# Bounds of the attention scores: one head per partition by way of DRAM instead of matmuls, a shift for each head, and a planner's allowance of 1.88

## The chip, the cores and the metric

The kernel runs on one NeuronCore of one Trainium2 chip. The metric is the device time of one execution in microseconds (us). Before the change three runs gave 1153.82, 1157.62 and 1160.69 us; the median is 1157.62 us. The core has five engines with a queue each: TensorE (PE in the profile, with its weight loads shown apart as PEld), VectorE (DVE), ScalarE (ACT), GpSimd (POOL) and SyncE (SP). An engine works through its own queue strictly in order. DMA transfers are issued from SP, POOL and ACT.

## The reference

Two independent layers are computed and their outputs are put side by side. A is a long convolution (an S4 layer); B is attention with 32 query heads that share one key and one value head.

```python
# A: u is 2048 x 576, 128 states per channel
K = einsum("dn,dnl,dn->dl", C, exp(dt * A * l), dt * B).real
ya = irfft(rfft(u, 4096) * rfft(K, 4096))[:2048] + u * Dskip
# B: x is 2048 x 576, H = 32 heads of 18
q = (x @ wq).reshape(2048, 32, 18)
k, v = x @ wk, x @ wv                 # 2048 x 18 each, shared by all heads
p = softmax(einsum("qhd,kd->hqk", q, k) * 18 ** -0.5)
yb = einsum("hqk,kd->qhd", p, v).reshape(2048, 576) @ wo
out = concatenate([ya, yb], axis=-1)
```

## The kernel before

**Attention** sets the frame. The 2048 queries are cut into 4 chunks c of 512; in a chunk come 8 groups g of 4 heads, in a group 16 blocks kb of 128 keys, and in a block two head pairs. That makes 1024 tiles of scores; two tiles (one key block of four heads) are called a step, so there are 512 steps, and a round of the main loop (`main`) takes three tiles. For each tile PE makes the scores `s` (L516) from a stacked fp16 query tile `aug` and the keys `kaug`, ACT turns them into `P = exp(s)` (L527, and L525 in the first group), and PE adds `P` times the values to `ops` (L823). At the end of a group DVE copies `ops` to `o`, which goes to DRAM as `od`; later it is divided by its sums and multiplied with `wo` (`op`, `outproj`, and at the very end `fin` in `finish`). A fin product that has not been started when the last scores are done is computed in `finish`, after the loop.

**Queries.** For each chunk five units m of up to 128 columns of `wq` (7, 7, 7, 7 and 4 heads) are projected on PE (`q`, L408). DVE splits the result into two fp16 halves `qh` and `ql` and takes the largest magnitude per column over the 512 queries, `ab` (L135). POOL stores the halves to the DRAM tensor `qd` (L458), from which SP fetches head pairs into the five `aug` buffers (L505).

**Bounds.** Softmax needs a shift that keeps exp in range. For a head, the sum over its 18 dimensions of max|q| times max|k| bounds every score. Before the change these sums run over partitions, since `ab` has a column of q per partition, and are done on PE: DVE builds a 128 x 128 tile `aw` out of `ab` and the key maxima `kmax` (L127), PE multiplies it with a 0/1 table `sel` into the PSUM tile `up` (L193; 8, 16 or 24 matmul records a unit), DVE reduces it to `un` (L135), takes the running maximum `u` over all units so far (L119), and spreads it into `sh`, which POOL stores as row 54 of `qd` (L496). All heads of a unit thus get one shift: the largest bound of any head so far. `kmax` itself comes from six instructions of PE and two of DVE in `bounds` (L374 to L387), called after round 2 of the main loop. The largest bound of all decides at the end, through `flag`, whether a slower general branch has to run.

**Convolution.** Its 576 channels are worked off in 12 pieces: DVE makes tables (`fr`, `tab`, L119 and L123), PE contracts them (`kg`, L1259) and transforms u and the kernel (`hu`, `lu`, `hk`, `lk`, `iy`, all L193), DVE multiplies (`us`, `ks`, `acc`, `pt`) and writes the result. Three times ACT computes a batch of sines and exponentials (`stage`).

**What sets the order.** PE, ACT and DVE run in the order in which the program was written, and a planner writes it: a `Clock` with estimated costs keeps one time for each of the three engines, and generators for the queries and bounds (`side`), the normalisation (`prepare`) and the convolution (`Conv`) yield what they want next: "v" for DVE work, "p" for PE work, in either case with the time from which it may go, and "w" to wait. `fill` puts pieces of such work between the attention's matmuls while a credit lasts. All PE pieces of this kind write to one single PSUM bank (`ps_f`, given out by `bank`), which the next piece can take only when DVE has read the last. `RATE` (1.84) is how many microseconds of the convolution's DVE work are allowed per step, `PACE` (1.79) the pace below which the convolution goes ahead of the queries. SP's and POOL's orders are made by a scheduler afterwards.

Two details matter for what follows. The first unit of chunk 0 is projected in `setup`, and its bounds wait until `bounds` has been called. The second one is projected in the main loop, after the bounds of the first.

## Time and profile before

| | |
|---|---|
| runs shown | 1153.82, 1157.62, 1160.69 us (median 1157.62) |
| profiled execution | 1154.84 us, of which the span from the first to the last instruction is 1153.0 us |
| granted TensorE clock, mean | 0.994 |
| busy in the span | PE 1080.8 us, ACT 998.7 us, DVE 995.5 us, POOL 141.4 us |
| DMA | 83.37 MB, mean 72 GB/s |

The page gives for each engine its busy time and share of the span. PE's busy time has modelled ends, so it is not work at PE's peak. A group line reads: line, engine, operation, output<-inputs, sizes, count | busy us in total, mean ns of one | idle time of the engine just before them, and what ended it. In the waits a row reads: who waited <- for whom: us in total, times, longest. A row of the timeline reads: start, duration, engine, line, operation, tiles, count, and in brackets the idle time before it with its cause; SPq is SP's queue issuing DMAs. All times are us from the start of the span.

### The profile page before, as it was taken

Reading aid. Unit: us, or ns where it says so; the run is one execution under the profiler, and the core shown is the slowest. Engines: PE = TensorE matmul, PEld = TensorE weight load, DVE = VectorE, ACT = ScalarE, POOL = GpSimd, SP = SyncE. Lnnn points to the kernel's source line nnn. Section 1 sums busy time; section 2 is a strip of 40 time slices with the busy share of each in tenths; the row PEclk is TensorE's granted clock in tenths of the full one; section 3 lists DMA queues with packets and bytes.
Section 4 is the critical chain, followed back from the end, with each engine's and each line's share of the span. In section 5 each row is a group of like instructions: output and inputs, shape, how many; then the busy total and the mean of one; then the engine's idle time right before and its main releaser. Section 6 shows DMA issues by size and latency. Waiting matters only on the chain.

```text
span 1153.0 us, 33069 instructions
## 1 busy us (share of the span) xinstructions
PE 1080.8 (94%) x13886; PEld 392.3 (34%) x13886; DVE 995.5 (86%) x1739; ACT 998.7 (87%) x1052; POOL 141.4 (12%) x257
## 2 busy tenths in 40 slices
PE   6999899999999999899999999999999999999998
PEld 2333323333334333324333333334323333323323
DVE  3788996998998998898899897987899899799693
ACT  3889988888888998998898999878999989899992
POOL 5320322012022000002032000001050000000000
PEclk9999999999999999999999999989999999999999
DMA  7412331114123102203122202102122200311201
GB/s 227 141 47 72 125 119 56 46 42 144 41 70 102 40 28 93 76 30 100 61 95 79 95 20 78 45 29 91 47 84 77 88 30 29 106 48 37 69 29 58
DMA packets 58895, 83.37 MB, mean 72 GB/s; under 512 B 14483, under 2 KB 34951, under 8 KB 58229
## 3 DMA queue, kind: packets, MB, share of 16 engines
q1 hardware_dynamic: 47173, 73.24, 19.4%
q0 software_dynamic: 10848, 7.37, 2.6%
q8 instruction: 111, 1.82, 0.6%
q10 hardware_dynamic: 720, 0.58, 0.2%
q14 instruction: 43, 0.35, 0.1%
HBM read 46.59 MB, written 33.85 MB: 70 GB/s over the span
## 4 chain that ended last, share of the span: by engine, by line
PE 59%; DVE 22%; ACT 11%; issue 6%; DMA 1%; SPq 0%; DVEq 0%; ACTq 0%
PE ops L823 24%; PE s L516 15%; ACT P L527 10%; PE op L193 5%; DVE tab L119 4%; PE q L408 4%; DVE ks L119 3%; PE iy L193 3%; PE kg L1259 3%; DVE acc L119 2%; DVE t L119 2%; PE hu L193 1%; DVE tt L119 1%; PE hk L193 1%; DVE fr L119 1%
## 5 line engine op out<-in xcount | busy, mean ns | idle before, releaser
L527 ACT ACTIVATE P<-s 128x1024 f32<-128x1024 f32 x992 | 934.5, 1033 | 111.9 <-PE s L516 109.7
L823 PE MATMUL ops<-P,v_sb 128*32 128x512 f32 x4096 | 508.7, 597 | 8.2 <-DVE o L123 7.8
L516 PE MATMUL s<-aug,kaug 55*128 55x512 f16 x2048 | 308.6, 382 | 37.2 <-ACT P L527 33.1
L516 PEld LDWEIGHTS <-kaug 55*128 55x128 f16 x2048 | 91.0, 94 | 371.3 <-issue 324.8
L823 PEld LDWEIGHTS ops<-P,v_sb 128*32 128x32 f32 x4096 | 116.6, 110 | 165.4 <-issue 128.4
L458 POOL DMA_DIRECT2D qd<-qh x116 | 65.6, 573 | 310.9 <-DVE qh L127 308.3
L408 PE MATMUL q<-x,wq_sb 128*32 128x256 f32 x1360 | 83.7, 382 | 0.1
L193 PE MATMUL op<-wo_sb,oT 126*32 126x288 f32 (+1 forms) x1080 | 78.5, 416 | 2.6 <-DVE ob L123 1.4
L119 DVE TENSOR_TENSOR tab<-tab,tt 128x576 f32<-128x576 f32 (+1 forms) x72 | 59.1, 821 | 1.4
L123 DVE COPY ksb<-kg 128x192 f32<-128x192 f32 x48 | 17.5, 364 | 48.2 <-PE kg L1259 48.0
L119 DVE TENSOR_TENSOR tab<-tab 128x576 f32<-128x576 f32 (+1 forms) x72 | 58.8, 817 | 0.0
L119 DVE TENSOR_TENSOR tt<-fr,sum 128x576 f32<-128x576 f32 (+1 forms) x72 | 58.8, 817 | 0.0
L119 DVE TENSOR_TENSOR tab<-fr,dif 128x576 f32<-128x576 f32 (+1 forms) x72 | 58.8, 817 | 0.0
L119 DVE TENSOR_TENSOR tab<-sum,fr 128x576 f32<-128x576 f32 (+1 forms) x72 | 58.8, 816 | 0.0
L408 PEld LDWEIGHTS q<-x,wq_sb 128*32 128x32 f32 x1360 | 39.4, 109 | 38.5 <-issue 13.7
L119 DVE TENSOR_TENSOR acc<-acc,pt 128x1728 f32<-128x1728 f32 (+2 forms) x36 | 48.6, 1351 | 0.1
L119 DVE TENSOR_TENSOR pt<-us,ks 128x1728 f32<-128x1728 f32 (+2 forms) x36 | 48.4, 1350 | 0.1
L1168 POOL MEMSET fr<- 128x192 f32 x24 | 12.0, 585 | 291.5 <-DVE tt L119 191.1
L193 PEld LDWEIGHTS op<-wo_sb,oT 126*32 126x32 f32 (+1 forms) x1080 | 30.6, 110 | 44.8 <-issue 19.1
L1259 PEld LDWEIGHTS kg<-tab 128*32 128x32 f32 x2304 | 35.8, 110 | 22.6 <-DVE ksb L123 7.6
L525 ACT ACTIVATE P<-s,bias 128x1024 f32<-128x1024 f32 x32 | 32.9, 1120 | 12.1 <-PE s L516 12.0
L1259 PE MATMUL kg<-tab 128*32 128x64 f32 x2304 | 41.7, 220 | 1.3 <-DVE tab L119 0.8
(160 smaller groups left out, 1021.0 us busy)
## 6 DMA issues: line engine op xcount, KB each, us to landing
od<-o SPq DMA_DIRECT2D x31, 256.0 KB
aug<-qd SPq DMA_DIRECT2D x124, 55.0 KB
u<-u SPq DMA_DIRECT2D x12, 384.0 KB
kd<-ksb SPq DMA_DIRECT2D x12, 384.0 KB
kt<-kd SPq DMA_DIRECT2D x48, 96.0 KB
outa<-u SPq DMA_DIRECT2D x12, 384.0 KB
pw<-pw SPq DMA_DIRECT2D x8, 528.0 KB
oT<-od SPq DMA_DIRECT2D x16, 252.0 KB
```

Of the source, the lines that this page charges most:

```text
L119: return self.v.tensor_tensor(out, *a, **k)
L123: return self.v.tensor_copy(out, *a, **k)
L193: nc.tensor.matmul(ps[j:e], w[:, j:e], x, start=start, stop=stop, tile_position=(0, j))
L408: nc.tensor.matmul(ps[o, 256 * f:256 * f + 256], w[:, k, i], xt[:, k, x], start=(k == 0), stop=(k == 4), tile_position=(0, 32 * j))
L458: q.dma_start(qd[h:h + n, row + d:row + d + nd, cs], src[i1:i1 + n * nd, :cs.stop - cs.start])
L516: nc.tensor.matmul(ps[:, j, :], self.kaug[r, kb * P:(kb + 1) * P], t[r, :], start=True, stop=True)
L525: nc.scalar.activation(pt, ps, AF.Exp, bias=self.bias, scale=SCALE / QQ)
L527: nc.scalar.activation(pt, ps, AF.Exp, scale=SCALE / QQ)
L823: nc.tensor.matmul(o_ps[32 * j:32 * j + 32, :], self.v[:, kb, :], pts[2 * n + j // 2][:, j % 2, :], start=(kb == 0), stop=(kb == 15), tile ...
L1168: nc.gpsimd.memset(t[:, :, 0:NF:8], one)
L1259: nc.tensor.matmul(ps[32 * g:32 * g + 32, d, :], t[:, :32], t[:, 32:], start=(j == 0), stop=(j == 1), tile_position=(0, 32 * g))
```

## The change

One head now lies on one partition. The column maxima `ab` of a unit (one float per partition) are written by SP to a row of a DRAM tensor `abd`, and POOL reads them back as `abh`, 7 (or 4) partitions of 18 floats: a head per partition. The key maxima make the same trip once (`kmd`, then `kmb`, spread to 8 partitions), and `bounds` reduces them to `kmh`, one row of 18 per partition. A unit's bounds are then four DVE instructions on at most 8 partitions: multiply `abh` by `kmh`, sum along the row into `un`, keep a running maximum in `umax`, and spread `un` to `sh`. Every head gets its own shift. The matmuls `up` and `kmx` are gone, and with them the units' `aw` and `kmax` (the first head group keeps its own in `setup`), and the bank `ps_f` is no longer used for bounds. At the end `umax` is brought to one partition through DRAM (`ud`, `uall`) and reduced for `flag`.

The generator of a unit now waits 9.0 planned microseconds after `ab` before it writes the four DVE instructions (`yield "v", K.v + 9.0, False`). `bounds` is called after round 4 instead of round 2, `side` projects the second unit of chunk 0 before the bounds of the first, and `RATE` and `PACE` are 1.88 and 1.82. In numbers of instructions: PE loses 166 (160 `up`, 6 `kmx`); DVE goes from 2082 to 2093; SP issues 31 more DMAs and POOL 21 more.

```diff
@@ -44,8 +44,8 @@
-RATE = 1.84
-PACE = 1.79
+RATE = 1.88
+PACE = 1.82
 AHEAD = 0.7
@@ -243,7 +243,10 @@
         self.v = cp.tile([P, 16, 32], F32, name="v_sb")
-        self.kmax = cp.tile([P, 5], F32, name="kmax")
+        self.kmax = cp.tile([P, 1], F32, name="kmax")
+        self.kmh = cp.tile([8, 32], F32, name="kmh")
+        self.umax = cp.tile([8, 1], F32, name="umax")
+        self.uall = cp.tile([1, 8], F32, name="uall")
         wkv = tp.tile([P, 5, 64], F32, name="wkv_sb")
@@ -275,7 +278,8 @@
         V.memset(self.v[:, :, DH:], 1.0)
-        self.ubound, self.bounded = None, False
+        V.memset(self.umax, 0.0)
+        self.abd, self.bounded = {}, False
         self.aug = {n: self.ring[n % NAUG] for n in range(64)}
@@ -359,11 +363,15 @@
             V.tensor_copy(dst, src)
-        V.tensor_scalar(km[:, 0:4], spread[:, 136:140], km[:, 4:5], None, op0=ALU.mult)
+        kmd = self.dr.tile([1, P], F32, tag="kmd", name="kmd")
+        nc.sync.dma_start(kmd.rearrange("o p -> p o"), km[:, 4:5])
         V.tensor_copy(self.v[:, :, :DH].rearrange("p (c j) d -> p c j d", j=4), vp.rearrange("p j (c d) -> p c j d", c=4)[:, :, :, :DH])
...
                 self.place(m, h2, l2, 32 * m - 32, (nc.sync, nc.sync))
+            if m == 2:
+                self.kmb = self.p1.tile([8, P], F32, tag="db", name="kmb", bufs=2)
+                nc.sync.dma_start(self.kmb, kmd[0:1, :].broadcast_to([8, P]))
             V.memset(self.wq[m][0:1, 0, 0:1], 0.0)
@@ -374,17 +382,9 @@
         nc, V, K = self.nc, self.V, self.k
-        km, spread = self.km, self.spread
         self.bounded = True
-        pk = self.bank(20, "kmx")
-        for m in range(5):
-            for b, n in ((0, 128),) if m < 4 else ((0, 64), (64, 64)):
-                nc.tensor.matmul(pk[b:b + n, 4 * m:4 * m + 4], spread[:, 2 * m:2 * m + n], km[:, 0:4], start=True, stop=True, tile_position=(0, b))
-        V.tensor_reduce(self.kmax, pk.rearrange("p (m c) -> p m c", c=4), axis=AX.X, op=ALU.max)
-        V.tensor_scalar(self.kmax, self.kmax, FLOOR, 1.002, op0=ALU.max, op1=ALU.mult)
-        K.pe(1.5)
-        K.v = max(K.v, K.t + 0.5)
-        K.fill = K.v + 0.25
+        V.tensor_reduce(self.kmh, self.kmb.rearrange("p (c d) -> p d c", c=4), axis=AX.X, op=ALU.max)
+        V.tensor_scalar(self.kmh, self.kmh, FLOOR, 1.002, op0=ALU.max, op1=ALU.mult)
@@ -446,18 +446,36 @@
             self.qd[c] = self.dr.tile([H, 55, CT], F16, tag="qd", name=f"qd{c}")
+            self.abd[c] = self.dr.tile([2, D], F32, tag="abd", name=f"abd{c}")
         qd = self.qd[c]
...
         n0 = 4 if (c, m) == (0, 0) else 0
+        m0, mn = MQ[m]
+        n = h1 - h0
+        abd = self.abd[c]
+        part = lambda f, i, j: abd[f:f + 1, i:j].rearrange("o p -> p o")
+        nc.sync.dma_start(part(0, m0, m0 + mn), ab[:mn, 0:1])
+        if m >= 3:
+            i = 504 if m == 3 else m0
+            nc.sync.dma_start(part(1, i, m0 + mn), ab[120 if m == 3 else 64:P, 0:1])
+        abh = self.p2.tile([8, 2, DH], F32, tag="abh", name=f"abh{c}_{m}")
+        nf = 1 if m < 4 else 2
+        def bound(q):
+            q.dma_start(abh[:n, :nf, :], abd[0:nf, h0 * DH:h1 * DH].rearrange("f (h d) -> h f d", d=DH))
...
             for row, src in ((0, qh), (18, qh), (36, ql)):
+                if row == 36:
+                    bound(q)
                 for i, h, n, d, nd in self.pieces(m, n0):
...
         def store_first(q):
+            bound(q)
             for row, part in ((0, 0), (18, 0), (36, 1)):
@@ -466,34 +484,21 @@
             yield "w", 0.0, False
-        aw = self.p2.tile([P, P], F32, tag="aw", name=f"aw{c}_{m}")
+        yield "v", K.v + 9.0, False
         ends = (FLOOR, ALU.max) if n0 else (TOP, ALU.min)
-        V.tensor_scalar(aw, ab[:, 0:1].broadcast_to([P, P]), ends[0], self.kmax[:, m:m + 1], op0=ends[1], op1=ALU.mult)
-        yield "p", max(K.v + (0.4 if self.due < self.step + 12 else SLACK), K.fill), False
-        up = self.bank(8, f"up{c}_{m}")
-        matmul4(nc, up, aw, self.sel[:, 8 * m:8 * m + 8], stop=(m == 0))
-        if m > 0:
-            n = 8 if m == 4 else 4
-            for b in range(0, n, 4):
-                matmul4(nc, up[:, b:b + 1], self.aw, self.sel[:, 39 + m:40 + m], start=False, stop=(b + 4 == n))
-        self.aw = aw
-        K.pe(0.1)
-        K.v = max(K.v, K.t + 0.3)
-        un = self.p2.tile([P, 1], F32, tag="un", name=f"un{c}_{m}", bufs=4)
-        V.tensor_reduce(un, up, axis=AX.X, op=ALU.max)
-        K.filled()
-        if self.ubound is not None:
-            u2 = self.p2.tile([P, 1], F32, tag="u2", name=f"u2_{c}_{m}", bufs=4)
-            V.tensor_tensor(u2, un, self.ubound, op=ALU.max)
-            un = u2
-        self.ubound = un
+        if m == 4:
+            V.tensor_tensor(abh[:n, 0, :], abh[:n, 0, :], abh[:n, 1, :], op=ALU.max)
+        V.scalar_tensor_tensor(abh[:n, 0, :], abh[:n, 0, :], ends[0], self.kmh[:n, 0:DH], op0=ends[1], op1=ALU.mult)
+        un = self.p2.tile([8, 1], F32, tag="un", name=f"un{c}_{m}", bufs=4)
+        V.tensor_reduce(un[:n, :], abh[:n, 0, :], axis=AX.X, op=ALU.add)
+        V.tensor_tensor(self.umax[:n, :], self.umax[:n, :], un[:n, :], op=ALU.max)
+        if (c, m) == (NCH - 1, 4):
+            ud = self.dr.tile([1, 8], F32, tag="ud", name="ud")
+            nc.sync.dma_start(ud.rearrange("o p -> p o"), self.umax)
+            nc.gpsimd.dma_start(self.uall, ud)
         sh = self.p2.tile([8, 256], F16, tag="sh", name=f"sh{c}_{m}", bufs=1)
-        V.tensor_scalar(sh, un[0:8, 0:1].broadcast_to([8, 256]), -1.0 / QS, -TOP, op0=ALU.mult, op1=ALU.max)
-        two = lambda t, n: t[:n, :].unsqueeze(1).broadcast_to([n, 2, 256])
-        nc.gpsimd.dma_start(qd[h0 + n0:h1, 54, :].rearrange("p (a n) -> p a n", a=2), two(sh, h1 - h0 - n0))
+        V.tensor_scalar(sh[:n, :], un[:n, 0:1].broadcast_to([n, 256]), -1.0 / QS, -TOP, op0=ALU.mult, op1=ALU.max)
+        nc.gpsimd.dma_start(qd[h0 + n0:h1, 54, :].rearrange("p (a n) -> p a n", a=2), sh[n0:n, :].unsqueeze(1).broadcast_to([n - n0, 2, 256]))
         self.queried = c * H + h1
@@ -692,8 +697,16 @@
         units = [(c, m) for c in range(NCH) for m in range(5)]
-        yield from self.queries(0, 0, None, None, self.ab0)
-        for c, m in units[1:]:
+        first, second = self.queries(0, 0, None, None, self.ab0), self.qproj(0, 1, self.x0)
+        yield next(first)
+        self.due = 16
+        for r in second:
+            yield r
+            if r[0] == "v":
+                break
+        yield from first
+        yield from second
+        for c, m in units[2:]:
             self.due = 16 * (8 * c + (0, 1, 3, 5, 7)[m])
@@ -854,7 +867,7 @@
                 self.settle(conv)
-            if r == 2 * NS:
+            if r == 4 * NS:
                 self.bounds()
@@ -892,7 +905,8 @@
         conv.drain()
-        nc.vector.tensor_scalar(flag, self.ubound[0:1, :], LIMIT / (2 * SCALE) * QQ, None, op0=ALU.is_le)
+        nc.vector.tensor_reduce(self.umax[0:1, :], self.uall, axis=AX.X, op=ALU.max)
+        nc.vector.tensor_scalar(flag, self.umax[0:1, :], LIMIT / (2 * SCALE) * QQ, None, op0=ALU.is_le)
         self.finish(NCH - 1, self.part, o_ps, self.w4, self.b4)
...

```

**PE, where the sum of unit 3 of chunk 0 (`up_3`) stood, 112 us after the start of the span.** Before:

```order
L516 LDWEIGHTS kaug
L516 MATMUL s_4_8_1464<-aug_114,kaug 128x512
L193 MATMUL up_3_1476<-sel_sb,aw_3_1079 32x8 x4
L193 MATMUL up_3_1476<-sel_sb,aw_2_827 32x1 x4
L823 MATMUL ops_2_1369<-P_4_5_1392,v_sb 32x512 x2
L823 MATMUL ops_2_1369<-P_5_5_1425,v_sb 32x512 x2
L823 MATMUL ops_2_1369<-P_4_6_1427,v_sb 32x512 x2
L823 MATMUL ops_2_1369<-P_5_6_1429,v_sb 32x512 x2
```

Now, at the same scores (`s_4_8`, head group 2, key block 8):

```order
L521 LDWEIGHTS kaug
L521 MATMUL s_4_8_1482<-aug_114,kaug 128x512
L193 MATMUL lk_1491<-kt_1166,dft_sb 32x192 x8
L836 MATMUL ops_2_1342<-P_4_4_1414,v_sb 32x512 x2
L836 MATMUL ops_2_1342<-P_5_4_1416,v_sb 32x512 x2
L521 LDWEIGHTS kaug
```

Between these scores and the next product two rows of `up` (8 matmul records in the first, 8 in the second) are gone; a transform of the convolution (`lk`) stands there, which before came one round earlier.

**DVE, between the column maxima of unit 3 of chunk 0 (`ab_3`) and their use.** Before, `aw_3` follows at once:

```order
L135 TENSOR_REDUCE ab_3_1066<-qh_3_1064 128x1
L127 TENSOR_SCALAR aw_3_1079<-ab_3_1066,kmax 128x128
L119 TENSOR_TENSOR tab_1_931<-tab_1_931 128x24x24
L119 TENSOR_TENSOR tab_1_931<-tab_1_931,tt_1_8_4_1048 128x24x24
L123 COPY ksb_597<-kg_1_0_1129 128x4x16x3
L123 COPY ksb_597<-kg_1_1_1159 128x4x16x3
L123 COPY scu_1193<-hu_1212 128x384
L119 TENSOR_TENSOR ab_499<-ab_499,dt_498 128x384
```

Now, `abh` being the maxima that came back from DRAM:

```order
L135 TENSOR_REDUCE ab_3_1051<-qh_3_1049 128x1
L123 COPY ksb_617<-kg_1_0_1091 128x4x16x3
L123 COPY ksb_617<-kg_1_1_1140 128x4x16x3
L123 COPY scu_1174<-hu_1201 128x384
L119 TENSOR_TENSOR ab_509<-ab_509,dt_508 128x384
L127 TENSOR_SCALAR ab_509<-ab_509 128x192
L119 TENSOR_TENSOR m_1176<-ab_509,pos_sb 128x1056
L119 TENSOR_TENSOR scu_1174<-lu_1218,scu_1174 128x384
L119 TENSOR_TENSOR scu_1174<-lu_1218,scu_1174 128x2x192
L131 SCALAR_TENSOR_TENSOR abh_3_1057<-abh_3_1057,kmh 7x18
L135 TENSOR_REDUCE un_3_1230<-abh_3_1057 7x1
```

Eight instructions of the convolution now stand between `ab_3` and the first that reads `abh`; five of them read a result of PE (`kg`, `hu`, `lu`).

**PE, the end of the program (`finish`).** Before:

```order
L193 MATMUL fin_14385<-wo_sb,oT_13148 32x288 x16
L193 MATMUL fin_14386<-wo_sb,oT_13148 32x288 x8
L669 MATMUL bc<-rc_last,b_14078 128x256
L193 MATMUL fin_14386<-wo_sb,oT_13148 32x288 x8
L193 MATMUL fin_14387<-wo_sb,oT_13148 32x288 x16
L193 MATMUL fin_14385<-w_14077,o_last 32x288 x8
L193 MATMUL fin_0_14451<-wo_sb,oT_13148 32x288 x8
L675 MATMUL bc<-rc_last,b_14078 128x256
L193 MATMUL fin_14386<-w_14077,o_last 32x288 x8
```

Now:

```order
L193 MATMUL fin_14277<-wo_sb,oT_12973 32x288 x8
L193 MATMUL fin_14278<-wo_sb,oT_12973 32x288 x8
L193 MATMUL fin_14279<-wo_sb,oT_12973 32x288 x8
L674 MATMUL bc<-rc_last,b_13972 128x256
L193 MATMUL fin_14279<-wo_sb,oT_12973 32x288 x8
L193 MATMUL fin_14277<-w_13971,o_last 32x288 x8
L193 MATMUL fin_0_14327<-wo_sb,oT_12973 32x288 x8
L680 MATMUL bc<-rc_last,b_13972 128x256
L193 MATMUL fin_14278<-w_13971,o_last 32x288 x8
```

`bc` waits for a reciprocal on DVE. Left to `finish` are 12 products of four matmuls out of `wo_sb` and `oT` instead of 17; the five others stand in the main loop, and the convolution's last `iy` stands at step 501 instead of 510.

## The prediction

> **What bounds the kernel now.** I read the totals of the page first, then the chain of work that ended last, then the waits of each engine, and last the timeline at the places that the change touches.
>
> ```profile
> PE 1080.8 (94%) x13886; PEld 392.3 (34%) x13886; DVE 995.5 (86%) x1739; ACT 998.7 (87%) x1052; POOL 141.4 (12%) x257
> PE 59%; DVE 22%; ACT 11%; issue 6%; DMA 1%; SPq 0%; DVEq 0%; ACTq 0%
> ...
> 60.00:1130.00 1070.00, 1014.69 (x13178) 368.39 (x13181) 950.92 (x1631) 958.59 (x1011) 114.90 (x205) 1.00 0.21 67
> ```
>
> PE is busy for 94% of the span and makes 59% of the chain. The third row is the stretch of the main loop (PE, PEld, DVE, ACT and POOL busy, then granted clock, DMA share, GB/s): of 1070 us PE is busy for 1015, DVE for 951, ACT for 959, and the clock is full. The three engines are close together, and the waits tell which one gives way:
>
> ```profile
> PE s L516 <- ACT P L527: 33.1, 92, 0.5
> PE ops L823 <- DVE o L123: 7.8, 10, 2.6
> PE iy L193 <- DVE ql L131: 3.3, 2, 2.9
> PE hu L193 <- DVE scu L119: 2.1, 2, 1.6
> ...
> ACT P L527 <- PE s L516: 109.7, 185, 4.2
> ...
> DVE ksb L123 <- PE kg L1259: 48.0, 34, 2.9
> ```
>
> ACT waits 109.7 us for PE, and PE only 33.1 us for ACT, 92 times in the 342 rounds of the loop. DVE's largest wait, 48.0 us, is for PE as well. PE's three largest waits for DVE come to 13.2 us. So PE sets the pace in about three rounds of four (250 of 342, 73%), ACT in the rest, and DVE rarely. A microsecond taken from PE inside the loop should bring about 0.73 us.
>
> **The change part by part.** *The matmuls `up`.*
>
> ```profile
> L193 PE MATMUL up<-sel_sb,aw 128*32 128x8 f32 (+1 forms) x320 | 6.0, 177 | 0.0
> L193 PEld LDWEIGHTS up<-sel_sb,aw 128*32 128x32 f32 x320 | 4.9, 110 | 7.1 <-issue 4.9 <-PE s L516 0.9 <-DVE ksb L123 0.5
> ...
> 53.61 0.22 PEld L193 LDWEIGHTS up<-sel_sb,aw 128*32 128x32 f32 x16 [0.23 <-issue]
> 53.73 0.17 PEld L823 LDWEIGHTS ops<-P,v_sb 128*32 128x32 f32 x8
> ...
> 73.49 0.16 PEld L823 LDWEIGHTS ops<-P,v_sb 128*32 128x32 f32 x8 [0.23 <-issue]
> ```
>
> At most the 20 units cost their weight loads and the idle time before them, 4.9 + 7.1 = 12.0 us. But at 53.61 us the sixteen loads delay the next product by 0.12 us only (53.73), and the 0.23 us before them stand in the same way before a product that follows the scores directly, at 73.49 us: that gap belongs to the end of the scores and stays. At least, then, 20 x 0.12 = 2.4 us; by the loads' busy time 4.9. I take the middle, 0.18 us a unit, 3.6 us, and 73% of it: **-2.6 us** (0 to -12.0).
>
> *The bank.* All side work of PE shares one PSUM bank, and `un` has to read `up` before the next piece starts. These waited for `un` (us, times):
>
> ```profile
>   PEld q L408: 1.3, 2
>   PEld hk L193: 1.2, 1
> ```
>
> That is 2.5 us of weight loads, some of it under matmuls that still run. I take half: **-1.2 us** (0 to -2.5).
>
> *The key maxima.*
>
> ```profile
> 32.61 1.27 PE L382 MATMUL kmx<-km,spread_sb 128*128 128x4 f32 x12
> 33.93 0.18 DVE L135 TENSOR_REDUCE kmax<-kmx 128x5 f32<-128x20 f32 x1 [3.49 <-PE kmx L382]
> 35.90 3.12 ACT L525 ACTIVATE P<-s,bias 128x1024 f32<-128x1024 f32 x3 [0.73 <-PE s L516]
> ```
>
> `kmx` holds PE for 1.27 us, and the exponentials behind it start 0.73 us late. DVE sat idle for 3.49 us before `kmax`; it will now run ahead with the convolution, which nobody waits for yet. **-0.7 us** (0 to -1.3). Its replacement reads `kmb` after round 4; SP issues `kmd` six transfers ahead of `kmb`, and behind these stand only loads for later.
>
> *DVE.*
>
> ```profile
> L127 DVE TENSOR_SCALAR sh<-u 8x256 f16<-8x256 f32 x19 | 5.7, 302 | 0.7
> L127 DVE TENSOR_SCALAR aw<-ab,kmax 128x128 f32<-128x128 f32 x20 | 5.7, 286 | 0.7
> L135 DVE TENSOR_REDUCE un<-up 128x1 f32<-128x8 f32 x20 | 3.2, 160 | 0.0
> L119 DVE TENSOR_TENSOR u<-un,u 128x1 f32<-128x1 f32 x18 | 2.9, 160 | 0.6
> ```
>
> A unit loses 0.286 + 0.160 + 0.160 + 0.302 = 0.91 us. It gains `sh` again and three instructions on rows of at most 18 elements, for which the nearest rows are the two of 160 ns: 0.302 + 3 x 0.160 = 0.78, with a fourth one (0.16) where m is 4. Over 20 units that is -1.9 us of DVE; with DVE's 22% of the chain, **-0.4 us** (0 to -1.9).
>
> *The way through DRAM.* A unit's maxima now go DVE, SP, DRAM, POOL, SBUF, and DVE waits in order for them: behind the first instruction that reads `abh` stand the convolution's, which release `kg`, `hu`, `lk` and `iy` on PE. One unit in the timeline shows the pieces:
>
> ```profile
> 65.90 3.46 POOL L458 DMA_DIRECT2D qd<-qh  x6 [8.23 <-DVE qh L127]
> 66.25 0.67 DVE L135 TENSOR_REDUCE ab<-qh 128x1 f32<-128x512 f16 x1
> 67.87 0.35 SPq L536 DMA_DIRECT2D od<-o  x1
> ...
> DMA to landing us min/median/max: 1.7/1.8/5.2
> ```
>
> The last row is for `sh`, the nearest small transfer. From the end of `ab` (66.92): SP issues in 0.35, landing 1.8, so 2.2 us; meanwhile POOL, which began at 65.90, must issue six stores (3.46 us) and two of `ql` at the same 0.58 each, and is ready at 70.5, 3.6 us after `ab`. Then 0.58 to issue and 1.8 to land: **6.0 us**. Against it stands the DVE work between `ab` and `abh` in the new order. It is least in unit 3 of chunk 0:
>
> ```profile
> L123 DVE COPY ksb<-kg 128x192 f32<-128x192 f32 x48 | 17.5, 364 | 48.2 <-PE kg L1259 48.0
> L123 DVE COPY scu<-hu 128x384 f32<-128x384 f32 x24 | 13.3, 555 | 13.8 <-PE hu L193 13.7
> L119 DVE TENSOR_TENSOR scu<-lu,scu 128x384 f32<-128x384 f32 x48 | 24.4, 550 | 2.9 <-PE lu L193 2.9
> L119 DVE TENSOR_TENSOR m<-ab,pos_sb 128x1056 f32<-128x1056 f32 (+2 forms) x7 | 7.6, 1094 | 0.0
> ```
>
> Two `ksb`, three `scu`, one `m` and two small ones: 2 x 0.36 + 0.56 + 2 x 0.55 + 1.09 + about 0.7 = 4.2 us, 1.8 short. But five of them read a result of PE and wait for it (a `ksb` that waits does so for 48.0 / 34 = 1.4 us), which fills most of that. Counted in the same way from the groups' means, the next shortest are 6.9 and 7.5 us, four lie from 9.0 to 10.1, twelve above 11. I take **+0.7 us** (0 to what the rival below costs). The 31 transfers more on SP (0.35 each, 11 us) and the 21 on POOL (0.58, 12 us, at 12% busy) hide there: POOL's other work is the units' own stores and a few memsets. SP works in order too, so a store of `ab` can stand behind a transfer that waits for another's landing, at worst this long:
>
> ```profile
> SPq L1283 <- DMA kd<-ksb: 33.9, 11, 4.6
> ```
>
> The Trainium skill speaks against this part. Its page "DMA: Bandwidth & Descriptors" (section "Rules for kernel authors") says that a non-contiguous last dimension becomes one descriptor per element, so the store of `ab` is 128 descriptors of 4 bytes; its section "Latency and other measured facts" gives an access to HBM as 0.2 us on average and 2 us at high load. The row of 1.7 / 1.8 / 5.2 agrees that the spread is wide. By that rule each of the two landings could take 1.8 us longer, an estimate from that page: 9.6 us in all. The shortfalls against 4.2, 6.9, 7.5 and 9.0 would then add up to 10.8 us, and the sum would end 4 us above today's time. By the row's median it ends 6 us below.
>
> *The end of the program.*
>
> ```profile
> 1137.09 2.58 PEld L193 LDWEIGHTS fin<-wo_sb,oT 126*32 126x32 f32 x48 [0.33 <-issue]
> 1137.54 1.75 DVE L674 RECIPROCAL rc_last<-rc_last 128x256 f32<-128x256 f32 x1
> 1142.08 0.30 PEld L675 LDWEIGHTS bc<-rc_last,b 128*128 128x128 f32 x2 [0.47 <-issue]
> ```
>
> Six products take 2.58 us, 0.43 each. Four of them and one further on are no longer there: the second `bc` can start near 1139.8, and the reciprocal it needs is done at 1139.29, so DVE does not become the bound. That is -2.1 us; the same five now stand in the loop, where 73% of 2.1 comes back, +1.6. **-0.5 us** (-2.1 to 0).
>
> *The allowance.* With 1.88 the convolution gets its DVE work earlier and ends nine steps sooner. No row prices a new order. PE's 13.2 us of waiting for DVE are what it can touch; I allow a third either way, 4 us, and take **-1.3 us**, a tenth, since PE's side pieces now change bank 20 times less.
>
> The sum: -2.6 - 1.2 - 0.7 - 0.4 + 0.7 - 0.5 - 1.3 = **-6.0 us**. The profiled execution took 1154.84 us (span 1153.0 and 1.84 around it), so 1148.8. It lies 2.8 us under the median of the runs shown, 1157.62; with the same step the forecast for the median is **1151.6 us**.
>
> **The rivals.** *ACT takes the gain.* If the freed time falls in rounds that already wait for ACT, only the key maxima and the end count: -0.7 - 0.5, about 1156.4. For it: 33.1 us of PE waiting for ACT. Against it: ACT's 109.7 us of waiting for PE.
>
> *DVE waits for its bounds.* The mechanism is the one instruction that reads `abh` in each unit. If both landings take the 5.2 us of the worst row, the way lasts 0.35 + 5.2 + 0.58 + 5.2 = 11.3 us, and the shortfalls of the 19 units after the first (against 4.2, 6.9, 7.5, 9.0 and so on) add up to 22 us. Without the +0.7 the rest is -6.7, so +15: 1173. Break-even lies near 8.4 us, where the shortfalls come to 6.7; at 9.6 us it would be 1162. For it: large transfers of other work stand just ahead in SP's order in several units. Against it: the median of 1.8, and DVE's idle time, which I have not counted in. The Trainium skill's page named above speaks for this case.
>
> *More than the sum.* The single bank is free more often, and DVE falls behind less: if half of the 13.2 us goes too, and the `up` units cost 4.9 rather than 2.6, the gain is about 6 + 6 + 2 = 14 us: 1144.
>
> **How the numbers follow.** About 0.5%, 5.8 us, is what a measurement of this kernel can tell from no change. The forecast (gain of 3 to 9 us, 1148 to 1155) has 0.50, of which 0.29 lies beyond 5.8 us and 0.21 within; more than the sum 0.17, all faster; ACT takes the gain 0.17, of which 0.14 is no change and 0.03 slower with an unlucky order; DVE waits 0.16, of which 0.15 is slower. Together faster 0.46, same 0.36, slower 0.18. The range of 1142 to 1164 leaves out the far ends of the second and third rival, about 2 in 10; the forecast's own range is 1148 to 1155.
>
> **What would show it.** The second head group starts here:
>
> ```profile
> 61.88 1.02 ACT L527 ACTIVATE P<-s 128x1024 f32<-128x1024 f32 x1
> ```
>
> Right: no `up` rows on PE; PE's busy time in the loop down by 3 to 6 us; ACT's wait for PE below 109.7; no row of the waits in which DVE waits for a DMA of `abh` with more than 2 us in all; `sh` in POOL's waits as before; the step from the last exponential to the end shorter by about 2 us. Wrong: DVE waiting for `abh` in several units, with `ksb`, `scu` or `sck` behind it and PE's waits for DVE up; or PE waiting for ACT by more than 33.1 us, with the span unchanged; or the exponentials of the second head group starting after 61.88 us because the maxima of the first two units come late behind the first loads.

## The result, and the profile after

| | before | after |
|---|---|---|
| runs in one comparison | 1153.82, 1156.56, 1157.62, 1160.69 us | 1193.93 to 1201.78 us |
| median | 1157.09 us | 1197.92 us |
| profiled execution (span) | 1154.84 us (1153.0) | 1193.93 us (1192.2) |
| mean granted TensorE clock | 0.994 | 0.987 |

The change makes the kernel slower: the ratio of after to before is 1.0358, with a 95% interval of 1.0338 to 1.0379. That is about 41 us where 6 us less were forecast, and the time lies 34 us above the end of the predicted range.

First the page of the profile after: the busy times (us, share of the span, instructions), and the chain that ended last by engine.

```profile
PE 1089.1 (91%) x13554; PEld 390.4 (33%) x13554; DVE 995.7 (84%) x1750; ACT 998.0 (84%) x1052; POOL 153.5 (13%) x278
PE 44%; DVE 23%; DMA 11%; ACT 11%; issue 7%; SPq 1%; POOL 1%; DVEq 0%; ACTq 0%; POOLq 0%
```

DVE and ACT have the work they had (995.7 and 998.0 us against 995.5 and 998.7), but a longer span to do it in. PE's share of the chain falls from 59% to 44%, and DMA's rises from 1% to 11%: transfers now stand on the path that sets the end. The waits of the engines say which (us in total, times, longest).

```profile
ACT P L532 <- PE s L521: 146.5, 197, 7.0
POOL abh L466 <- DMA abd<-ab: 75.3, 14, 8.7
PE s L521 <- ACT P L532: 42.0, 110, 1.0
DVE abh L131 <- DMA abh<-abd: 17.2, 7, 5.0
PE ops L836 <- DVE o L123: 14.8, 11, 5.3
DVE abh L119 <- DMA abh<-abd: 11.0, 4, 4.3
POOL qd L475 <- DMA qd<-qh: 10.8, 5, 3.6
PE kg L1273 <- DVE ksb L123: 4.3, 1, 4.3
```

DVE waits 17.2 + 11.0 = 28.2 us for `abh`, 11 times. POOL stands 75.3 us for the landing of `abd`. Behind DVE, PE waits for `o` (14.8 us, before 7.8) and for `ksb` (4.3 us); both wait longer for each other too, ACT for PE 146.5 us (before 109.7), PE for ACT 42.0 (33.1). The critical chain in order of time gives how long single transfers were on the path (start, us, what).

```profile
142.83 9.42 DMA abd<-ab
152.80 5.55 DMA abh<-abd
175.24 8.07 DMA abd<-ab
183.84 3.00 DMA abh<-abd
...
591.06 9.32 DMA qd<-qh
...
714.12 8.35 DMA abd<-ab
```

A store `abd<-ab`, 128 elements of 4 bytes, takes 8 to 9.4 us from its issue to its landing. The timeline of the unit at 142.83 us shows what that does (start, us, engine and line, output<-inputs, idle before and what ended it; a row of SP, one of POOL and three of DVE).

```profile
142.83 0.33 SPq L458 DMA_DIRECT2D abd<-ab  x1
...
152.80 0.53 POOL L466 DMA_DIRECT2D abh<-abd  x1 [7.49 <-DMA wo_sb<-wo]
...
142.13 0.67 DVE L135 TENSOR_REDUCE ab<-qh 128x1 f32<-128x512 f16 x1
...
152.90 0.51 DVE L119 TENSOR_TENSOR fr<-t,t 128x192 f32<-128x192 f32 x1
158.37 0.17 DVE L131 SCALAR_TENSOR_TENSOR abh<-abh,kmh 7x18 f32<-7x18 f32 x1 [4.96 <-DMA abh<-abd]
```

`ab` is there at 142.80. DVE has work until 153.41, 10.6 us, as the planner meant it. But POOL can issue the load only at 152.80 (the landing of `abd` is at 142.83 + 9.42 = 152.25, and in the unit at 714.12 us the load also follows the landing by 0.5 us; the profile names `wo_sb`, which landed last by its account), and `abh` is there at 158.35. The way takes 15.5 us here. Over the 18 units from the third on, from the end of `ab` to the landing of `abh`, it takes 10.2 to 15.5 us, 11.5 in the median (landings from the times at which the sixteen parts of a transfer report in the trace).

The end of the program did what it was to do. ACT's timeline, first of the kernel before (the last exponential), then of the changed one (the first of the second head group and the last):

```profile
1131.38 1.02 ACT L527 ACTIVATE P<-s 128x1024 f32<-128x1024 f32 x1 [0.61 <-PE s L516]
```

```profile
65.06 1.02 ACT L532 ACTIVATE P<-s 128x1024 f32<-128x1024 f32 x1 [0.90 <-PE s L521]
...
1172.82 1.02 ACT L532 ACTIVATE P<-s 128x1024 f32<-128x1024 f32 x1 [0.46 <-PE s L521]
```

From the last exponential to the end of the span it was 1153.0 - 1132.4 = 20.6 us, now it is 1192.2 - 1173.84 = 18.4, 2.2 less. So the whole loss is ahead of it. Compared by the start of each head group, 8.2 us are lost by the third and 30.1 by the 13th (13 of the 20 units are made by then), 1.5 more in the next four, beside which two units are made, and the rest from there on, where the last five are made.

### The profile page after: what moved, and what is told of

It is laid out like the page before. It is cut to its first block, busy times and chain, and to the rows that moved or that the text cites. A ratio compares the mean times of both kernels' runs of the same rounds, so it can differ in the third digit from the quotient of the medians.

```text
span 1192.2 us, 32502 instructions
## 1 busy us (share of the span) xinstructions
PE 1089.1 (91%) x13554; PEld 390.4 (33%) x13554; DVE 995.7 (84%) x1750; ACT 998.0 (84%) x1052; POOL 153.5 (13%) x278
## 4 chain that ended last, share of the span: by engine, by line
PE 44%; DVE 23%; DMA 11%; ACT 11%; issue 7%; SPq 1%; POOL 1%; DVEq 0%; ACTq 0%; POOLq 0%
PE ops L836 19%; PE s L521 12%; ACT P L532 10%; DMA abd<-ab 4%; DVE ks L119 4%; DVE tab L119 4%; PE op L193 3%; DVE acc L119 3%; DMA abh<-abd 3%; PE kg L1273 2%; PE q L408 2%; PE iy L193 2%; DVE pt L119 2%; DVE t L119 2%; DMA qd<-qh 2%
## 5 line engine op out<-in xcount | busy, mean ns | idle before, releaser
L532 ACT ACTIVATE P<-s 128x1024 f32<-128x1024 f32 x992 | 934.1, 1034 | 151.4 <-PE s L521 146.5
L836 PE MATMUL ops<-P,v_sb 128*32 128x512 f32 x4096 | 514.6, 601 | 15.2 <-DVE o L123 14.8
L521 PE MATMUL s<-aug,kaug 55*128 55x512 f16 x2048 | 312.6, 382 | 51.5 <-ACT P L532 42.0
L1273 PEld LDWEIGHTS kg<-tab 128*32 128x32 f32 x2304 | 36.4, 111 | 31.9 <-issue 11.3
```

The lines of the kernel that those rows point to most:

```text
L521: nc.tensor.matmul(ps[:, j, :], self.kaug[r, kb * P:(kb + 1) * P], t[r, :], start=True, stop=True)
L532: nc.scalar.activation(pt, ps, AF.Exp, scale=SCALE / QQ)
L836: nc.tensor.matmul(o_ps[32 * j:32 * j + 32, :], self.v[:, kb, :], pts[2 * n + j // 2][:, j % 2, :], start=(kb == 0), stop=(kb == 15), tile ...
L1273: nc.tensor.matmul(ps[32 * g:32 * g + 32, d, :], t[:, :32], t[:, 32:], start=(j == 0), stop=(j == 1), tile_position=(0, 32 * g))
```

## The experiments

All times are medians; ratios are to the kernel before, run on the same chip in the same comparison, with 95% intervals. Expectations stand as they were written before the runs.

### Without DVE's wait, without the load, without the store

Three kernels on top of each other, all of which leave the true bounds out. In the first, DVE reads a constant:

```diff
+        self.abc = cp.tile([8, 2, DH], F32, name="abc")
+        V.memset(self.abc, 16.0)
...
-        V.scalar_tensor_tensor(abh[:n, 0, :], abh[:n, 0, :], ends[0], self.kmh[:n, 0:DH], op0=ends[1], op1=ALU.mult)
+        V.scalar_tensor_tensor(abw[:n, :], abw[:n, :] if m == 4 else self.abc[:n, 0, :], ends[0], self.kmh[:n, 0:DH], op0=ends[1], op1=ALU.mult)
```

> All transfers of the changed kernel stay, but DVE reads its maxima from a constant tile (16.0 in every place, near what the real ones are) instead of abh, so it never waits for the way through DRAM; the bounds are left out of the computation. Three theories of the 40 us. W, the waiting: DVE stands 28.2 us in order behind abh, and what it should have released comes late; then this kernel ends at 1150 to 1160 us. J, the jam: the stores of 128 times 4 bytes hold the 16 DMA engines for some 6 us a unit (in the trace of the change their own landing takes 8.1 us in the median, and that of the qd<-qh stores beside them went from 2.8 to 7.6 us), so everything else that the units store and fetch comes late; then it stays above 1180 us. O, the order: the new allowance and the second unit's earlier place cost by themselves; then it stays above 1180 us as well.

In the second the load goes too, in the third the store:

```diff
-            q.dma_start(abh[:n, :nf, :], abd[0:nf, h0 * DH:h1 * DH].rearrange("f (h d) -> h f d", d=DH))
+            pass
...
-        nc.sync.dma_start(part(0, m0, m0 + mn), ab[:mn, 0:1])
```

> As the one with the constant tile, and the load abh<-abd is left out too, so POOL no longer stands waiting for the landing of abd (75.3 us in the change) ahead of the last ql store and of sh. The stores abd<-ab stay. W: as the first, 1150 to 1160. If POOL's waiting is a part of the loss, this one is 3 us or more faster than the first. J: the qd<-qh stores still land after 7 us, and the time is as that of the first, above 1180. O: above 1180.

> As the last, and the stores abd<-ab are left out too: no transfer of the way through DRAM is left but those of the key maxima and the one at the end. W: as the two others, 1150 to 1160. J: 1150 to 1160, 20 us or more below the two others, and the qd<-qh stores land after 2.8 us again. O: still above 1180. My own estimate of the prediction for this kernel is its sum without the way through DRAM, -6.7 us from the profiled execution before: 1148 to 1151.

| kernel | median | ratio | step |
|---|---|---|---|
| after | 1197.92 us | 1.0358 (1.0338 to 1.0379) | |
| DVE reads a constant | 1180.68 us | 1.0215 (1.0175 to 1.0255) | -16.5 us |
| and no load | 1180.20 us | 1.0209 (1.0171 to 1.0247) | -0.7 us |
| and no store | 1163.30 us | 1.0057 (1.0043 to 1.0072) | -17.6 us |

(A step is the difference of the ratios times 1156.4 us; by the ratios' intervals the three steps are known to some 5, 6 and 5 us.) None of the three theories holds alone. DVE's waiting is 16.5 us of the loss, the store by itself 17.6, and with neither the kernel is still 6.6 us slower than before. POOL's 75 us of standing cost nothing that can be measured. So the store costs time even when nobody waits for what it carries: the jam. The landings in the five traces show what it slows (median from issue to the last of the sixteen reports, us; an empty field: no such transfer):

| | `abd<-ab` | `qd<-qh` | `kmd<-km` |
|---|---|---|---|
| before | | 2.8 | |
| after | 8.1 | 7.6 | 7.6 |
| DVE reads a constant | 8.5 | 8.1 | 9.0 |
| and no load | 8.5 | 8.3 | 8.7 |
| and no store | | 2.8 | 8.8 |

The first of the sixteen parts of an `abd` store often reports 1.4 or 1.5 us after the issue, the last after 8; and POOL's stores of q, which have nothing to do with it, report just as late. In the unit at 714.12 us POOL's store of 713.07 has all its reports by 714.73; the seven issued after it, up to 716.88, have their last between 721.4 and 723.9, and the `abd` store has its last at 722.47. The trace lists the 4-byte packets of that store with 9 ns each and all within 2.4 us of its issue, so it is the reports that come late. The Trainium skill, page "DMA: Bandwidth & Descriptors", section "Queues, rings and completion order", says that the increment of a semaphore lands only after every earlier write of that DMA engine, across its queues. The trace agrees: SP's store holds up the reports of POOL's, 7.6 to 8.3 us beside it against 2.8 without. Through which wait this becomes 17.6 us is not shown: in the traces of the last two kernels ACT's wait for PE goes from 124.2 to 117.9 us, and no other wait of PE, ACT or DVE changes by more.

### Rows instead of elements

```diff
-                self.p2.tile([P, 2], F32, tag="ab", name=f"ab{c}_{m}"))
+                self.abs[m % 2])
...
-            self.abd[c] = self.dr.tile([2, D], F32, tag="abd", name=f"abd{c}")
+            self.abd[c] = self.dr.tile([2, D, 8], F32, tag="abd", name=f"abd{c}")
...
-        part = lambda f, i, j: abd[f:f + 1, i:j].rearrange("o p -> p o")
-        nc.sync.dma_start(part(0, m0, m0 + mn), ab[:mn, 0:1])
+        part = lambda f, i, j: abd[f, i:j, :]
+        nc.sync.dma_start(part(0, m0, m0 + mn), ab[:mn, :])
```

`self.abs` are two tiles of 8 columns, of which the first is used; `abh` has the 8 columns too.

> The whole computation, with rows of 32 bytes in place of single elements: ab is a tile of 8 columns of which only the first is used, abd holds 8 numbers for each dimension, and store and load move whole rows. Bytes go from 512 to 4096 a store; the number of rows that a store writes stays at 128. If the small size of each write is what takes the 8.1 us, abd lands in 2 to 3.5 us, the way is 6 to 8 us, DVE's wait for abh falls below 8 us and the time to 1150 to 1165 (by W and J alike). If the number of rows is what counts, the landing stays near 8 us and the time near 1198.

1165.58 us, ratio 1.0073 (1.0048 to 1.0098). `abd` lands in 2.8 us (median), `qd<-qh` in 2.9. The waits of this kernel that name the way through DRAM:

```profile
POOL abh L469 <- DMA abd<-ab: 9.8, 4, 4.8
DVE abh L131 <- DMA abh<-abd: 1.7, 1, 1.7
DVE abh L119 <- DMA abh<-abd: 1.4, 2, 0.9
```

3.1 us of DVE's waiting are left of 28.2. So the number of rows, still 128, isn't it. In rows the way takes 6.7 us (median of the same 18 units), near the 6.0 that had been forecast. With eight times the bytes, 33 of the 41 us are gone (0.0285 of the ratio).

### Elements, but apart

The kernel without the load, with 64 bytes from one element to the next:

```diff
-            self.abd[c] = self.dr.tile([2, D], F32, tag="abd", name=f"abd{c}")
+            self.abd[c] = self.dr.tile([2, D, 16], F32, tag="abd", name=f"abd{c}")
-        part = lambda f, i, j: abd[f:f + 1, i:j].rearrange("o p -> p o")
+        part = lambda f, i, j: abd[f, i:j, 0:1]
```

> The kernel with the constant tile and without the load abh, whose stores abd<-ab put each element of 4 bytes 64 bytes from the next, so that no two fall into one piece of 64 bytes. The bounds are left out as in the other. Z, the size: a write of 4 bytes costs what it costs wherever it lands, so abd lands after 8 us again, qd<-qh after some 8, and the time is 1180. N, neighbours: the writes hinder each other because they fall into the same pieces, so abd lands in 2 to 4 us and the time is 1163 to 1166.

1162.26 us, ratio 1.0047 (1.0030 to 1.0065). `abd` lands in 2.9 us, `qd<-qh` in 2.9. The same 128 writes of 4 bytes whose reports took 8 us cost nothing that can be measured when they do not lie side by side (two runs of this kernel; without the store it was 1163.30 us): it is the neighbours, not the size. SP, which works in order, stands for `ab` ahead of these stores; it does so as long in the kernel without the load (first row) as here (second row), so that is not what the store costs:

```profile
SPq L460 <- DVE ab L135: 139.1, 15, 28.5
SPq L460 <- DVE ab L135: 144.2, 15, 28.1
```

Rows of 32 bytes, and of 16 in the next section, touch each other and are fast too. So the distance from one write's start to the next may be what counts; where the border lies for single elements, between 4 bytes and 64, wasn't tried.

### The key maxima, and the allowance

Even without any store of `ab` the start was late. Two views of the kernel without the store, SP and ACT in time:

```profile
27.35 0.41 SPq L369 DMA_DIRECT2D kmd<-km  x1
27.82 8.82 SPq L356 DMA_DIRECT2D kaug<-keys  x6
...
37.88 1.11 ACT L528 ACTIVATE P<-s,bias 128x1024 f32<-128x1024 f32 x1 [3.00 <-PE s L519]
44.25 23.21 ACT L528 ACTIVATE P<-s,bias 128x1024 f32<-128x1024 f32 x23 [5.25 <-PE s L519]
```

`kmd` is one more store of 128 neighbouring elements, and behind it on SP come the keys that the first scores need; ACT stands 3.00 and 5.25 us. So the next kernel writes `kmd` in rows of 16 bytes:

```diff
-        kmd = self.dr.tile([1, P], F32, tag="kmd", name="kmd")
-        nc.sync.dma_start(kmd.rearrange("o p -> p o"), km[:, 4:5])
+        kmd = self.dr.tile([P, 4], F32, tag="kmd", name="kmd")
+        nc.sync.dma_start(kmd, km[:, 1:5])
```

> The kernel with rows of 32 bytes, and the key maxima take their way in rows too: kmd is written in 128 rows of 16 bytes in place of 128 elements of 4, and kmb reads all of it. In the kernels with the constant tile and with rows of 32 bytes the first exponentials still stand idle for 3.0 and 5.3 us while kaug<-keys goes out behind kmd (in the kernel before: 0.7 and 0.5), and the second head group starts 5.3 to 5.6 us late. K, the store of the key maxima does it: then the second head group starts within 2 us of 61.9 us and the time falls by 5 to 7 us, to 1158 to 1161. If it is the later place of the bounds or the order of the first two units: the start stays late and the time at 1165.

1162.35 us, ratio 1.0049 (1.0037 to 1.0061). By the ratios that is 2.8 us less than with rows for `ab` alone, known to 3 us, so it may be nothing; I had expected 5 to 7, and the two traces differ by 6.6 (spans of 1166.0 and 1159.4 us). `kmd` lands in 1.5 us (8.5 in the kernel with rows for `ab` alone), and the start is mended:

```profile
27.81 4.47 SPq L358 DMA_DIRECT2D kaug<-keys  x6
...
37.14 23.21 ACT L534 ACTIVATE P<-s,bias 128x1024 f32<-128x1024 f32 x23 [1.46 <-PE s L525]
60.29 1.02 ACT L536 ACTIVATE P<-s 128x1024 f32<-128x1024 f32 x1
```

The second head group starts at 60.29 us, 1.6 before the 61.88 of before; the third is 1.9 us behind again. Then the allowance, in both directions: this kernel with `RATE` and `PACE` set back, and the kernel before with nothing but the new ones.

```diff
-RATE = 1.88
-PACE = 1.82
+RATE = 1.84
+PACE = 1.79
```

> As the last, with the allowance of before (1.84 and 1.79). If 1.88 and 1.82 cost by themselves, this one is 3 us or more below the last, 1152 to 1157; if the allowance is worth what the prediction gave it, it is 1 us above the last; if it does nothing, they are the same.

> The kernel before with nothing changed but the allowance, 1.88 and 1.82. The prediction gave the allowance -1.3 us (4 either way): 1155 to 1156. If the allowance is what keeps the kernel without the way through DRAM 7 us above before: 1160 to 1164.

Set back: 1180.44 us, ratio 1.0212 (1.0196 to 1.0228), 18 us worse, which none of the three expectations held. The kernel before with 1.88: 1158.36 us, ratio 1.0020 (1.0008 to 1.0031), so 2.3 us slower. The first has its reason at the end, DVE and ACT in time:

```profile
1140.21 2.56 DVE L119 TENSOR_TENSOR acc<-us,ks 128x2304 f32<-128x2304 f32 x1
...
1160.83 0.55 DVE L119 TENSOR_TENSOR u<-u,iy 128x384 f32<-128x384 f32 x1 [1.83 <-PE iy L193]
...
1140.48 1.02 ACT L536 ACTIVATE P<-s 128x1024 f32<-128x1024 f32 x1 [0.46 <-PE s L525]
1162.03 0.38 ACT L668 ACTIVATE o_last<-ops 128x256 f32<-128x256 f32 x1 [20.53 <-DVE rc_last L667]
```

The last piece of the convolution lies behind the last exponential (1141.5 us) and holds DVE for 20 us ahead of the normalisation. In the order of the changed kernel the convolution needs the larger allowance; in the order of before it does not, and the kernel pays a little for it.

### The place of the bounds in the order

Six us were open now. First the wait of the generator, shorter:

```diff
-        yield "v", K.v + 9.0, False
+        yield "v", K.v + 5.0, False
```

> The kernel with rows for bounds and key maxima (1162.4 us), and DVE's instructions on the bounds stand 5 us behind the stores in the order instead of 9. B, blocked side work: a unit keeps the side stream while it waits for its bounds, so no projection is there to fill PE's free time (PE waits 41.1 us for ACT and ACT 122.3 us for PE, against 33.1 and 109.7 before, though PE has less to do); then 4 us less of it bring 2 to 4 us: 1158 to 1160, unless DVE then waits for abh by more than 10 us. If the blocking does nothing: 1162, or slower by DVE's waits.

1169.50 us, ratio 1.0115 (1.0090 to 1.0140): 7.6 us worse. DVE's two rows of waiting for `abh` come to 21.3 us:

```profile
DVE abh L131 <- DMA abh<-abd: 10.7, 5, 4.2
DVE abh L119 <- DMA abh<-abd: 10.6, 3, 5.3
```

In rows the way takes 6.7 us here too (median), more than the 5. Next, the old order of the first two units, without the wait for the first unit's bounds, and on top of it a stream of its own for the bounds:

```diff
-        first, second = self.queries(0, 0, None, None, self.ab0), self.qproj(0, 1, self.x0)
...
+        yield from self.queries(0, 0, None, None, self.ab0)
+        for c, m in units[1:]:
...
-            if r == 4 * NS:
+            if r == 2 * NS:
```

> The kernel with rows for bounds and key maxima, with the order of the first units and the place of the key maxima as in the kernel before (the first unit whole, then the second; maxima after round 2), and no wait for the first unit's bounds, which have long landed. S, the start: in the kernel with rows the first unit's shifts go out at 54.6 us (before: 42.2), its aug tiles are fetched from 56.9 (before: from 47.5), and ACT stands 3.8 us at 61.3; then this kernel's second head group is done 2 to 4 us earlier and the time is 1158 to 1160. If the rest of the loop decides alone: 1162.

```diff
-        yield "v", K.v + (0.0 if n0 else 9.0), False
+        self.pending.append(self.shift(c, m, n0, abh, K.v + (0.0 if n0 else 9.0)))
...
-                for st in (prep, side, conv) if urgent else (prep, conv, side):
+                for st in (low, prep, side, conv) if urgent else (low, prep, conv, side):
```

> As the last, and the bounds of a unit wait in a stream of their own, so the next unit's projection goes on while a unit waits for its bounds. B and S together: ACT's wait for PE falls to 110 us or less, PE's for ACT to 34, and the time to 1150 to 1156, below the kernel before. If the unevenness has another cause: 1158 to 1162.

> As the last, with the allowance of before (1.84 and 1.79). In the kernel with rows the smaller allowance left the convolution unfinished behind the last exponential, for 16 us more. If the blocked side work was the reason for that, this one ends within 2 us of the last; if the way through DRAM needs the larger allowance in any case, it is 10 us or more above it.

1171.73, 1185.12 and 1191.35 us, ratios 1.0135 (1.0111 to 1.0159), 1.0247 (1.0224 to 1.0269) and 1.0302 (1.0280 to 1.0324). All three miss. The start of the kernel with its own stream, SP, DVE and ACT in time:

```profile
43.31 0.52 SPq L462 DMA_DIRECT2D abd<-ab  x1
...
52.19 0.18 DVE L131 SCALAR_TENSOR_TENSOR abh<-abh,kmh 7x18 f32<-7x18 f32 x1 [17.81 <-DMA abh<-abd]
...
61.98 3.13 ACT L551 ACTIVATE P<-s,bias 128x1024 f32<-128x1024 f32 x3 [19.10 <-PE s L542]
```

I had taken the first unit's bounds for long landed, since its `ab` is there at 15 us. But SP comes to that store only at 43.31, behind the keys, the weights and the first loads of the convolution. That the changed kernel projects the second unit first hides this. So the same kernels once more, with this one store ahead of `kmd` (at 27 us) and the load behind POOL's first stores (the kernel with rows alone is among them, and it too without the wait for the first unit's bounds):

```diff
+        self.abd[0] = self.dr.tile([2, D, 8], F32, tag="abd", name="abd0")
+        nc.sync.dma_start(self.abd[0][0, 0:P, :], ab)
         kmd = self.dr.tile([P, 4], F32, tag="kmd", name="kmd")
```

> The kernel with rows for bounds and key maxima (1162.4 us), with the first unit's maxima stored right ahead of those of the keys (at 27 us; so far SP came to them at 43.8, behind loads of the weights and of the convolution) and loaded behind POOL's first stores; DVE's instructions on the first unit's bounds wait no longer than for the key maxima. If the start is what is left of the loss: the second head group's end comes 3 to 4 us earlier and the time is 1158 to 1159. If the loop is: 1161 to 1163.

> The kernel with the old order of the first units and the old place of the key maxima (1171.7 us), with the first unit's maxima stored early as well. Its loss against the kernel with rows was DVE's wait of 11.6 us for the first unit's bounds at the start; that goes: 1158 to 1161. If it stays above 1168, the old order itself costs.

> The kernel whose bounds wait in a stream of their own (1185.1 us), with the first unit's maxima stored early. There ACT stood 19.1 us at 43 to 62 us, while DVE waited 17.8 us for the first unit's bounds; from the first to the 24th head group that kernel then won 6 us against the kernel before, and lost 14 in the 25th, where DVE's copy o came 11.7 us late. With the start mended: 1160 to 1166; below 1157 only if the 25th group's stall goes too.

> As the last, with the allowance of before (1.84, 1.79). The convolution's last part then lies behind the last exponential as in the other two with this allowance, which cost 8 to 16 us, but the stall of the 25th group lies elsewhere: 1160 to 1172.

| kernel | median | ratio |
|---|---|---|
| rows, early store | 1161.03 us | 1.0039 (1.0024 to 1.0054) |
| rows, old order of the first units, early store | 1162.67 us | 1.0057 (1.0039 to 1.0076) |
| the last with its own stream | 1169.30 us | 1.0113 (1.0095 to 1.0132) |
| the last with 1.84 and 1.79 | 1175.80 us | 1.0168 (1.0149 to 1.0187) |

The start is mended by it in all (in the old order 9 us come back, with the own stream 16), but it is hardly more than 1 us of what was open, and the own stream does not help, with the old allowance still less. The last three lie above the ranges that I had given them, which ended at 1161, 1166 and 1172 us. The kernel in rows with the early store is the best one with the way through DRAM, and it is still 4.5 us behind the kernel before.

### The matmuls alone, and the place alone

The last two leave the transfers out of it. One takes nothing but the matmuls `up` (320 records in the profile) from the kernel before (`un` is reduced from a constant tile); the other also puts DVE's instructions where the change has them, with its allowance, and drops the planner's slot for the matmuls.

```diff
-        up = self.bank(8, f"up{c}_{m}")
-        matmul4(nc, up, aw, self.sel[:, 8 * m:8 * m + 8], stop=(m == 0))
...
+        K.pe(0.0, K.fill)
+        up = self.upc
```

> The kernel before without the 320 matmuls up: un is reduced from a constant tile of the same size, so the bounds are left out of the computation. Every other instruction of PE, DVE and ACT stands where it stood. This prices the terms up (-2.6 us, 0 to -12.0) and bank (-1.2, 0 to -2.5) by themselves: 1152 to 1154 us by the prediction; 1150 or less by the rival of more than the sum; 1156 to 1157 if ACT takes the gain.

```diff
+        yield "v", K.v + 9.0, False
         aw = self.p2.tile([P, P], F32, tag="aw", name=f"aw{c}_{m}")
...
-        yield "p", max(K.v + (0.4 if self.due < self.step + 12 else SLACK), K.fill), False
```

> As the last, and DVE's instructions on the bounds stand 9 us behind the stores in the order, where the changed kernel has them, with the allowance of 1.88 and 1.82; the key maxima and the first two units stay as before, and no transfer goes through DRAM. If the new place in the order takes the gain back: 1158 to 1162, like the mended kernels, with PE waiting some 41 us for ACT. If the place is harmless: 1153 to 1156, and what is left of the loss lies in the transfers and the start.

Without the matmuls: 1155.62 us, ratio 0.9988 (0.9974 to 1.0003). That is 1.4 us (3.0 to none) for what was to bring 3.8. The page's busy times, and what PE and ACT wait for each other:

```profile
PE 1080.2 (94%) x13566; PEld 389.7 (34%) x13566; DVE 995.5 (86%) x1739; ACT 998.4 (87%) x1052; POOL 141.5 (12%) x258
```

```profile
ACT P L524 <- PE s L513: 110.6, 184, 3.1
...
PE s L513 <- ACT P L524: 33.9, 95, 0.5
```

PE loses 0.6 us of busy time (1080.8 before; clocks of 0.995 and 0.994), not 6.0, and the two waits are those of before (109.7 and 33.1). In the one execution that each trace holds, the 2nd to the 13th head group start 0.6 to 0.8 us later than in the kernel before, and the last one and the end of the loop 0.8 to 0.9: between these two executions nothing was won in the loop.

With the new place: 1164.53 us, ratio 1.0085 (1.0059 to 1.0111), 11 us above the last (0.0097 of 1156 us), of which the allowance alone gave 2.3 in the kernel before. It lies above the 1158 to 1162 that I had expected of a harmful place. If the two simply add, about 9 us (5 to 13 by the intervals) are left for writing the same DVE instructions 9 planned us later, without one transfer. The mark I had set for it, PE waiting 41 us for ACT, is not there; ACT's wait for PE is what rises:

```profile
ACT P L519 <- PE s L508: 119.5, 200, 4.8
PE s L508 <- ACT P L519: 34.6, 92, 1.9
```

110.6 in the kernel without the matmuls, 119.5 here. The generator of a unit also makes the next unit's projection; while it waits, PE lacks that work, and later has it in a heap. That is a reading that fits, but it is not shown. The stream of its own, which should have shown it, with the early store loses 14 us in the 25th head group, where DVE's copy `o` comes 11.7 us late. From the start of the second head group to that of the 24th its trace does better, 0.6 us won against the kernel before, where the kernel with rows and the early store alone loses 3.7.

```profile
PE ops L854 <- DVE o L123: 14.2, 6, 11.7
```

This row is of the kernel with its own stream and the early store. So why the later place costs stays open; that it does is shown for the kernel before.

## Why the prediction was wrong, point by point

**The way through DRAM (+0.7 us) is the step that failed.** It had 6.0 us for the way, with 1.8 us for each landing from the row of `sh`. The load did land in 2.1 us (median; 1.6 to 5.5). The store took 8.1: 128 neighbouring elements of 4 bytes are not a small transfer like `sh`. The way took 11.5 us, and DVE's waits add up to 28.2 us in 11 places. DVE's work between `ab` and `abh` had been counted rightly where it was least: 4.2 us in unit 3 of chunk 0, and 4.4 in the trace. There DVE also waits 7.7 us for PE, reaches `abh` 11.7 us after `ab` and does not wait for it. In the 18 units it comes to `abh` 9.6 to 13.6 us after `ab`: that would have covered 6.0 and does not always cover 10.2 to 15.5. The effect of DVE's waits on the time is 16.5 us by the run with the constant, where +0.7 had been put down.

**The rival "DVE waits for its bounds" was right for 16.5 of the 41 us.** It had 11.3 us for the way, 22 us of shortfalls and 1173. Its mechanism holds, its reason does not: two landings of 5.2 us each was not what happened, and that 11.3 comes so near to 11.5 is luck. It also lacked the second half, the 17.6 us that the store costs by itself, beside transfers that nobody had connected with it. POOL's 12% and SP's 11 us priced the issuing engines; the sixteen DMA engines behind them had no term in the sum.

The Trainium skill's page "DMA: Bandwidth & Descriptors" (sections "Rules for kernel authors" and "Latency and other measured facts") had been cited as speaking against this part, for an estimate of 9.6 us of way; the measured 11.5 is nearer to that than to 6.0. The reason taken from there, one descriptor per element and 2 us for each access under load, would have slowed both landings by 1.8 us; the load took 2.1 us and only the store was slow, so the way came near for another reason.

**The matmuls and the bank (-2.6 and -1.2 us)** measured -1.4 us together (-3.0 to +0.3), where -3.8 had been put down: too large a gain. The 0.18 us a unit, taken from the weight loads' rows, and the factor of 73% were applied to instructions without which PE's busy time fell by 0.6 us.

**The key maxima (-0.7 us)** came as a loss: some 3 us (0 to 6) hang on the slow form of `kmd`. SP had behind it not "only loads for later" but six transfers `kaug<-keys` that the first scores need. With `kmd` in rows the second head group starts 1.6 us earlier than before, which fits the sign of the term, though the third is late again.

**The end of the program** came 2.2 us earlier, -2.1 had been worked out. Whether the five products cost 1.6 us in the loop, as estimated, no run shows by itself.

**The allowance (-1.3 us)**: +2.3 us (0.9 to 3.6) in the old order; in the new one it is needed, 18 us hang on it. The estimate of a tenth of PE's waits had no ground in either.

**What had no term:** the new place of the bounds in the order, some 9 us in the kernel before. The prediction counted whether DVE would have enough to do in between, and not what else moves with the place. The parts do not simply add up: with rows and the early store all of it together is 4.5 us.

Of the signs named in advance, those for "wrong" were there: DVE waits for `abh` in several units, `ksb` and `o` behind it, and the second head group starts at 65.06 us instead of 61.88. Of those for "right" only the end was, beside the absent rows of `up`. PE's busy time rose by 8.3 us where it was to fall by 3 to 6; in the kernel without the store, with the same 13554 matmuls, it is 1079.5 us at a mean clock of 0.996, after the change 1089.1 at 0.987. The granted clock falls where the unit shown above stands. Two stretches of the changed kernel, from 138 to 158 us and from there to 200 (length, busy times of PE, PEld, DVE, ACT and POOL, then the clock, the DMA share and GB/s):

```profile
138.00:158.00 20.00, 14.62 (x106) 3.14 (x94) 15.20 (x25) 16.85 (x19) 4.85 (x9) 0.91 0.69 127
158.00:200.00 42.00, 37.50 (x460) 13.13 (x456) 38.00 (x74) 34.05 (x37) 6.83 (x12) 0.96 0.28 84
```

0.91 and 0.96 against 1.00 in the kernel before between 150 and 200 us. So some of the loss is a lower clock beside the stalls. The trace gives the order in time: from the second head group to the last exponential of the changed kernel the granted clock is at half in five stretches of 3.4 or 6.8 us, and each begins 1.9 to 3.6 us after PE has come to a stop for 2.0 to 5.3 us (the first stop at 148.5 us, the first such stretch at 151.8). In the kernel before there is one such stretch in that part (6.8 us), in the kernel without the store none. Not every stop is followed by one (2.9 us at 359.1 is not), and no run tests it.
